# Fused linear attention and two MoE layers on one core: y of a step in one go, a new order of issue, and eight low parts moved to VectorE

## The chip, the cores and the metric

The kernel runs on one core of a Trainium2 chip. The metric is the device time of one execution in microseconds. Three executions of the kernel before took 455.67, 456.74 and 457.1 us, so the median is 456.74 us. The trace shown here is of a further execution of 458.59 us, whose span from the first to the last instruction is 456.7 us; 1.9 us lie around the span.

Five engines are named: PE (TensorE, matmuls; PEld is its loading of weights), DVE (VectorE), ACT (ScalarE), POOL (GpSimd) and SP (SyncE, which here only issues DMAs).

## The reference

Three layers follow each other, all in float32.

```
# 1. attention with a decaying state: batch 2, 8 heads, 768 positions, head_dim 48
for t in range(768):
    y[t]  = r[t] @ (state + (u*k[t]) outer v[t])
    state = w[t][:, None] * state + k[t] outer v[t]
x = y as 1536 tokens x 384
# 2. dense layer ("MoE1"): 384 -> 2048 -> 384
x = silu(x @ w_in) @ w_out
# 3. routed layer ("MoE2"): 8 experts, top 1, 384 -> 1024 -> 384
out[i] = gate[i] * (relu(x[i] @ w1[e]) @ w2[e])     e = argmax(x[i] @ w_gate)
```

## The kernel before, in words

**Attention.** The 1536 tokens are cut into 12 steps of 128 positions, the two batches alternating (step n belongs to batch n % 2). One step makes, from running products of w, scaled keys `kh` and scaled queries `rh`, and then: `kp` transposes kh, `Kt` copies it out of PSUM, `U` is keys times values, `sc` are scores between positions, `cp` and `cq` copy the scores under the mask into `A` (even and odd heads, written before with the diagonal by `Ad` and `Ae`), `Sb` updates the state, and `y` (three column groups j = 0, 1, 2) sums the part from the old state `Tb` and the part from `A`. `xh` and `xl` split y into a high and a low part. The tiles of w, of the running products (`QF`), of rk, kh, rh and Tb exist once, so a step reuses what the step before has read.

Up to now the y of a step was issued in two pieces: the token `y` (group 0: 16 matmuls from the third step on) and the token `z` (groups 1 and 2: 40 matmuls), with other work between them.

**The layers.** Tokens go through MoE1 in six chunks of 256, two attention steps each. A chunk is 8 units; a unit is `s1_` (18 matmuls into a PSUM bank), `gh` and `sg` (ACT: silu, twice), `gl` (DVE: low part) and `s2_` (12 matmuls that add into the chunk's sums). Every product is made of three passes: high x high, high x low, low x high. MoE1's 16 weight pieces come as 64-bit floats and are decoded: `drw` loads one, `wx` shifts its low word (L350 on ACT or L352 on DVE, as the letter in `L3` says), `wy` (DVE, L356), `wt` (ACT, L360) and `wo` (DVE, L364) build the float, `wh` (ACT, L368) rounds the high part and `wl` (L372, POOL or DVE as `LO` says) makes the low part. Four buffers hold pieces that are being decoded.

MoE2's weights come as float32: ACT rounds the high part (L386) and DVE or POOL subtracts it for the low part (L387). The first pieces are converted while MoE1's last chunk runs.

**Routing.** For each finished chunk c, `ra` and `rd` copy its sums into rows, `jk` (16 of them, DVE, L476) are the dot products with the gate's weights, `rt` finds the expert, `cu` (PE) counts, `ru_` (`gates`) makes slots and gate values, and `rs` (POOL) scatters the rows.

**What sets the order.** The string `PLAN` lists the work of PE, ACT, DVE and POOL in the order in which each engine takes it, from the start until MoE1's unit 31 of 48; a colon gives the PSUM banks. SP's loads keep the order in which they stand there too. What comes after PLAN (the rest of MoE1, MoE2) is put in order by the framework's scheduler from its own estimates; `REST` says which leftovers of routing are handed in at which slot there. Each engine takes its instructions strictly in order, so one that waits holds up all that stand behind it.

In the loop over units 32 to 47, `ensure(m, lo)` converts MoE2's pieces up to m; `lo` is the engine of the low parts. In the last chunk (`c == NCH - 1`) it is called at units i = 1, 2, 3 (pieces 0 to 7) and 4, 5 (pieces 8 to 11).

Of the kernel before, what the change touches and what calls it, by code (L numbers as in the profile page):

```python
# [36 lines left out]

L3 = "DAADADADADADADDA"  # L40
# [3 lines left out]
PLAN = """
dw0 drk0 dvv0 Qs0 drw0 pd0 PC0 kh0 Fs0 kp0:0 dw1 Kt0 ru0 drk1 jq0 U0:1 rh0 wx0 dvv1 dp0:2 Sb0 drw1 wy0 sc0:34 dg0 wt0 Qs1 Ad0 wo0 dw2 PC1 pd1 ru1 Ae0
drk2 cp0 y0:5 wh0 Fs1 dp1:6 wx1 cq0 wl0 z0 jq1 kh1 rh1 kp1:7 xh0 dvv2 dg1 wy1 Ad1 sc1:01 dtk2 xl0 Kt1 Qs2 Ae1 drw3 U1:2 cp1 wt1 pd2 cq1 PC2 y1:3 tk2
Sb1 z1 wo1 xh1 xl1 wh1 Fs2 s1_0:4 wl1 jq2 kh2 dw3 rh2 dg2 drk3 Tb2 kp2:6 Ad2 wx3 sc2:57 wy3 gh0 dvv3 Ae2 Qs3 dtk3 s1_1:0 sg0 cp2 Kt2 drw2 wt3 gl0 cq2
PC3 wo3 drw5 pd3 tk3 wh3 U2:1 gh1 y2:2 sg1 Sb2 wx2 wl3 z2 gl1 drw4 dg3 Fs3 lc xh2 s2_0:36 Ad3 drw7 xl2 jq3 kh3 rh3 kp3:4 Ae3 Tb3 sc3:57 wy2 dw4 Kt3
drk4 wx5 wx4 U3:1 cp3 wy5 y3:0 dvv4 wt2 cq3 dtk4 wt5 Sb3 z3 wo2 wo5 xh3 wh2 xl3 wh5 wl2 s1_8:2 wl5 drw6 wy4 s1_2:4 gh8 wx7 tk4 wt4 drw9 sg8 s2_1 gl8
gh2 wo4 sg2 wx6 gl2 s1_9:5 wy7 Qs4 wh4 s1_10:7 wt7 dg4 wl4 pd4 gh9 wx9 PC4 sg9 Ad4 wo7 s2_8:10 drw8 gl9 wh7 Fs4 Ae4 s1_3:2 wl7 gh10 jq4 kh4 drw11 s2_2  # L50
rh4 sg10 Tb4 wx8 gl10 wy6 kp4:4 sc4:57 wy9 gh3 Kt4 wy8 sg3 U4:4 wt6 gl3 wt9 cp4 Sb4 wt8 cq4 y4:2 wo6 s1_11:4 wo9 wh6 wo8 wh9 z4 wl6 wh8 s2_9 wx11 wl9
xh4 drw10 xl4 wl8 s1_4:5 gh11 drw13 wy11 sg11 gl11 wt11 s2_3 wo11 wx10 drw12 s1_5:7 gh4 wy10 wh11 wx13 sg4 s2_10 wl11 wt10 gl4 drw14 wo10 wx12 s2_4
wy13 gh5 wy12 s1_12:2 wh10 sg5 wl10 wt13 gl5 s2_11 wx14 wt12 wo13 drw15 gh12 sg12 wo12 wh13 s1_6:4 gl12 wh12 wl13 dw5 wl12 s1_13:5 drk5 gh6 wy14 sg6
wx15 gl6 dvv5 s2_5 Qs5 dtk5 wt14 wy15 s1_7:7 PC5 gh13 wo14 wt15 pd5 sg13 kh5 wh14 s2_12 gl13 tk5 kp5:2 gh7 wo15 s2_13 Kt5 sg7 Fs5 wh15 gl7 wl14 U5:4
jq5 dg5 s1_14:5 Ad5 dw6 wl15 Ae5 rh5 s2_6 Tb5 drk6 gh14 Sb5 sg14 Qs6 sc5:27 dvv6 gl14 PC6 dtk6 cp5 s2_7 pd6 cq5 Fs6 y5:4 ra0 s1_15:5 kh6 jq6 rd0 tk6
dw7 z5 gh15 sg15 dg6 kp6:2 rh6 xh5 s2_14 Ad6 gl15 drk7 xl5 Kt6 Tb6 Ae6 sc6:73 Qs7 dvv7 U6:6 dtk7 cp6 PC7 s1_16:5 pd7 cq6 Sb6 Fs7 y6:4 gh16 s1_17:2 kh7
sg16 jq7 tk7 gl16 dw8 z6 gh17 sg17 dg7 kp7:7 xh6 gl17 s2_15 Ad7 xl6 rh7 Kt7 Tb7 drk8 Ae7 sc7:36 Qs8 ra1 U7:5 cp7 dvv8 PC8 s1_18:2 rd1 dtk8 cq7 Sb7 pd8
y7:4 kh8 gh18 s2_16:71 Fs8 sg18 gl18 tk8 jq8 z7 dw9 kp8:0 xh7 rh8 s1_19:3 Kt8 xl7 drk9 dg8 Tb8 Ad8 sc8:65 Qs9 dvv9 gh19 U8:2 dtk9 Ae8 cp8 s2_17 pd9
sg19 Sb8 PC9 gl19 cq8 y8:0 Fs9 s1_20:4 kh9 jq9 tk9 z8 dw10 gh20 sg20 kp9:2 xh8 gl20 s2_18 Kt9 xl8 rh9 dg9 drk10 sc9:36 Tb9 Ad9 Qs10 U9:5 dvv10 Ae9 cp9
s1_21:4 dtk10 Sb9 PC10 cq9 pd10 y9:2 kh10 gh21 s2_19 Fs10 sg21 gl21 tk10 jq10 z9 dw11 kp10:0 rh10 xh9 s1_22:5 Kt10 dg10 drk11 xl9 Ad10 Tb10 sc10:36  # L60
Qs11 dvv11 gh22 Ae10 U10:4 dtk11 cp10 sg22 s2_20 pd11 PC11 cq10 lw0 gl22 Sb10 s1_23:0 Fs11 lf0 kh11 jq11 s2_21 tk11 gh23 sg23 gl23 kp11:2 y10:3 dg11
Kt11 s1_24:6 jk0_0 Ad11 jk0_1 lw1 jk0_2 Ae11 jk0_3 z10 jk0_8 jk0_9 gh24 jk0_10 lf1 sg24 U11:5 rh11 xh10 s2_22 gl24 xl10 Tb11 jk0_4 sc11:40 Sb11 jk0_5
s1_25:2 cp11 jk0_6 cq11 y11:6 jk0_7 gh25 s2_23 jk0_11 sg25 jk0_12 gl25 jk0_13 z11 jk0_14 ra2 jk0_15 rd2 s1_26:3 xh11 rt0 xl11 jk1_0 cu0:5 gh26 jk1_1
s2_24:40 sg26 ru_0 s1_27:2 gl26 rs0 jk1_2 jk1_3 jk1_4 s2_25 gh27 jk1_5 jk1_6 sg27 jk1_7 gl27 s1_28:7 jk1_8 jk1_9 jk1_10 jk1_11 s2_26 gh28 jk1_12 sg28
jk1_13 jk1_14 gl28 s1_29:1 jk1_15 rt1 s2_27 gh29 jk2_0 jk2_1 sg29 jk2_2 gl29 cu1:6 jk2_3 s1_30:5 ru_1 s2_28 gh30 jk2_4 rs1 jk2_5 sg30 jk2_6 gl30
s1_31:3 jk2_7 jk2_8 jk2_9 jk2_10 s2_29 gh31 jk2_11 sg31 jk2_12 jk2_13 gl31 s1_32:2 jk2_14 jk2_15 rt2 s2_30 gh32 sg32 gl32 cu2:7 s1_33:1 ru_2 s2_31
"""
# [1091 lines left out]
```

## Time and profile before

| | |
|---|---|
| median of three runs | 456.74 us |
| profiled execution | 458.59 us, span 456.7 us |
| PE busy | 427.9 us, 94% of the span |
| DVE busy | 307.4 us, 67% |
| ACT busy | 229.3 us, 50% |
| POOL busy | 150.8 us, 33% |
| mean granted PE clock | 0.963 |

A line of the chain that ended last, or of a timeline, begins with the start in us from the span's start and a duration in us. In lists of groups the number after the bar is the sum in us, and the next one the mean duration of one in ns. Matmuls overlap: from one to the next counts the difference of their starts, not the duration. PE's granted clock has two levels: 1.00 stands for 2.4 GHz and 0.50 for 1.2 GHz.

### The profile page before, as it was taken

The page shows a single profiled execution, that of the slowest core. Times are in us where ns is not written, and L with a number is a line of the kernel's source. Part 1 is how long each engine was busy: PE and PEld are TensorE (multiplying, and loading weights), DVE is VectorE, ACT ScalarE, POOL GpSimd, SP SyncE. Part 2 cuts the span into 40 slices and gives each one's busy share as a digit, 9 for nine tenths or more (in the row PEclk, how much of TensorE's full clock was granted, in tenths as well). Part 3 has the DMA queues.
Part 4 walks back from the last instruction along what each step waited for, and adds up shares of the span by engine and source line. Part 5 has one row for each costly group of instructions (what it writes and reads, how often), then busy time and mean ns, then how long its engine had stood idle before and what let it go on. Part 6 is the DMA issues. An engine that isn't in the chain of part 4 may idle for free.

```text
span 456.7 us, 9042 instructions
## 1 busy us (share of the span) xinstructions
PE 427.9 (94%) x3551; PEld 406.9 (89%) x3551; DVE 307.4 (67%) x618; ACT 229.3 (50%) x438; POOL 150.8 (33%) x152
## 2 busy tenths in 40 slices
...
GB/s 270 389 155 164 154 202 148 254 186 194 195 133 130 104 152 183 135 35 36 3 35 36 1 69 209 165 187 243 244 207 255 205 201 245 213 112 27 0 32 33
DMA packets 20772, 67.83 MB, mean 149 GB/s; under 512 B 3042, under 2 KB 7293, under 8 KB 20720
## 3 DMA queue, kind: packets, MB, share of 16 engines
...
q14 instruction: 22, 0.18, 0.1%
...
## 4 chain that ended last, share of the span: by engine, by line
PE 62%; DVE 14%; issue 10%; DMA 7%; POOL 3%; ACT 2%; SPq 0%; POOLq 0%; DVEq 0%; ACTq 0%
PE s L400 27%; PE acc L429 23%; DMA rawd<-wd 4%; DVE jk L476 3%; PE acc L550 3%; PE y L304 3%; PE sc L273 2%; DVE rawd L364 2%; DVE QF L200 2%; POOL wt L372 1%; DMA tk<-tk 1%; PE U L288 1%; PE kp L261 1%; DVE A L278 1%; DMA rk<-rk 1%
## 5 line engine op out<-in xcount | busy, mean ns | idle before, releaser
L400 PE MATMUL s<-xh,wt 128*128 128x256 f32 x960 | 156.8, 286 | 4.4 <-DVE gl L420 2.7
L429 PE MATMUL acc<-wt,gh 128*128 128x384 f32 x576 | 149.7, 342 | 3.1 <-POOL wt L372 2.4
L400 PEld LDWEIGHTS s<-xh,wt 128*128 128x128 f32 x960 | 135.0, 191 | 7.0 <-DVE gl L420 2.9
L406 ACT ACTIVATE gh<-s 128x512 fp32r<-128x512 f32 x80 | 47.9, 598 | 125.3 <-PE s L400 115.0
L429 PEld LDWEIGHTS acc<-wt,gh 128*128 128x128 f32 x576 | 101.6, 190 | 4.5 <-POOL wt L372 2.6
L429 PE MATMUL acc<-wt,gl 128*128 128x384 f32 x288 | 95.9, 338 | 0.0
L400 PE MATMUL s<-xl,wt 128*128 128x256 f32 x480 | 84.1, 284 | 0.8 <-DVE xl L332 0.7
L387 POOL TENSOR_TENSOR wt<-raw,wt 128x768 fp32r<-128x768 f32 x34 | 64.4, 1900 | 60.6 <-ACT wt L386 60.5
L400 PEld LDWEIGHTS s<-xl,wt 128*128 128x128 f32 x480 | 69.1, 191 | 1.4 <-DVE xl L332 1.2
L386 ACT CAST wt<-raw 128x768 fp32r<-128x768 f32 x64 | 52.7, 834 | 15.9 <-PE acc L429 11.9
L429 PEld LDWEIGHTS acc<-wt,gl 128*128 128x128 f32 x288 | 54.4, 190 | 0.3 <-DVE gl L420 0.3
L420 DVE TENSOR_TENSOR gl<-s,gh 128x512 fp32r<-128x512 f32 x48 | 32.9, 686 | 31.4 <-ACT s L409 31.0
L387 DVE TENSOR_TENSOR wt<-raw,wt 128x768 fp32r<-128x768 f32 x30 | 33.8, 1131 | 26.2 <-ACT wt L386 25.9
L422 DVE SCALAR_TENSOR_TENSOR gl<-s,gh 128x512 fp32r<-128x512 f32 x32 | 22.1, 691 | 38.9 <-ACT gh L406 38.8
L476 DVE SCALAR_TENSOR_TENSOR jk<-xr,wgr 128x384 f32<-128x384 f32 x80 | 46.9, 640 | 0.0
L204 POOL TENSOR_TENSOR tk<-tk 128x384 f32<-128x384 f32 x10 | 12.2, 1219 | 72.1 <-DMA tk<-tk 56.0
L252 ACT ACTIVATE A<-ident,dg 128x128 f32<-128x128 f32 x96 | 30.4, 393 | 3.6 <-DVE dg L243 2.7
...
L409 ACT ACTIVATE s<-s 128x512 f32<-128x512 f32 x48 | 28.4, 593 | 0.0
L372 POOL TENSOR_TENSOR wt<-rawd,wt 128x768 fp32r<-128x768 f32 x5 | 11.4, 2289 | 46.6 <-ACT wt L368 46.6
L304 PE MATMUL y<-A,vv 128*32 128x128 f32 x384 | 17.8, 286 | 4.4 <-DVE A L278 3.6
L278 DVE COPY_PREDICATED A<-mask,sc 128x512 f32<-128x512 int32 x24 | 17.5, 728 | 5.2 <-PE sc L273 5.0
...
## 6 DMA issues: line engine op xcount, KB each, us to landing
...
```

The costliest lines, as they stand in the source:

```text
L252: nc.scalar.activation(out=d["A"][:, h], in_=ident, func=AF.Copy, scale=d["dg"][:, h:h + 1])
L278: nc.vector.copy_predicated(d["A"][:, h::2], bc(mask.bitcast(I32).unsqueeze(1), [128, 4, 128]), d["sc"][h])
L304: nc.tensor.matmul(d["y"][ps_, j], l, r, start=i == (1 if n < B else 0), stop=i == len(a[j]))
L386: nc.scalar.copy(t[:, 0], r)
L387: lo.tensor_tensor(out=t[:, 1], in0=r, in1=t[:, 0].bitcast(F32), op=ALU.subtract)
L400: nc.tensor.matmul(s[:, fi], wv[:, a, k, fi * 128:fi * 128 + 128], x[b][:, k], start=n == 0, stop=n == 8)
L406: lz["sg"] = nc.scalar.activation(out=gt[u][0], in_=gt[u][2], func=f)
L409: lz["sg"] = nc.scalar.activation(out=gt[u][2], in_=gt[u][2], func=AF.Silu)
L420: nc.vector.tensor_tensor(out=gl, in0=s, in1=gh.bitcast(F32), op=ALU.subtract)
L422: nc.vector.scalar_tensor_tensor(out=gl, in0=s, scalar=0.0, in1=gh.bitcast(F32), op0=ALU.max, op1=ALU.subtract)
L429: lz["s2"] = nc.tensor.matmul(acc[j][:, 0:DM], g[a][:, fi, j * 128:j * 128 + 128], w[:, b, fi * DM:fi * DM + DM], start=first and fi == 0 ...
L476: nc.vector.scalar_tensor_tensor(out=jk, in0=ro[c]["xr"][j][:, 0:DM], scalar=1.0, in1=wgr[e // 4][:, e % 4], op0=ALU.mult, op1=ALU.mult, a ...
```

## The change

1. From the third step on (`ONE_Y = 2`) the token `y` issues all 56 matmuls of a step's y; the tokens z2 to z11 are gone.
2. `PLAN`, `REST` and `BANKS` are new. The attention's step 4, which stood among the decoding of MoE1's weights, now comes after it, so that steps 4 to 11 stand where steps 5 to 11 stood. On PE, s2_0 stands behind kp3, sc3 and U3, and U2 stands ahead of s1_1. On DVE, Fs2 stands ahead of xl1, Fs3 ahead of gl0, and wy2, wy5 and wx4 ahead of xl3. SP's loads for step 4 come after the last of MoE1's weights. The last dot products, expert choice and gates of chunk 2 (jk2_15, rt2, cu2, ru_2) go from PLAN to REST.
3. `L3` is D throughout: the shift `wx` of all 16 pieces is made by DVE (eight were made by ACT).
4. `ensure(2 * i + 1)` at units 1 to 3 of the last chunk: the low parts of MoE2's pieces 0 to 7 are made by DVE (POOL made them).

```diff
-L3 = "DAADADADADADADDA"
+RUN = 2
+
+ONE_Y = 2
+
+L3 = "DDDDDDDDDDDDDDDD"
...
-Sb1 z1 wo1 xh1 xl1 wh1 Fs2 s1_0:4 wl1 jq2 kh2 dw3 rh2 dg2 drk3 Tb2 kp2:6 Ad2 wx3 sc2:57 wy3 gh0 dvv3 Ae2 Qs3 dtk3 s1_1:0 sg0 cp2 Kt2 drw2 wt3 gl0 cq2
-PC3 wo3 drw5 pd3 tk3 wh3 U2:1 gh1 y2:2 sg1 Sb2 wx2 wl3 z2 gl1 drw4 dg3 Fs3 lc xh2 s2_0:36 Ad3 drw7 xl2 jq3 kh3 rh3 kp3:4 Ae3 Tb3 sc3:57 wy2 dw4 Kt3
-drk4 wx5 wx4 U3:1 cp3 wy5 y3:0 dvv4 wt2 cq3 dtk4 wt5 Sb3 z3 wo2 wo5 xh3 wh2 xl3 wh5 wl2 s1_8:2 wl5 drw6 wy4 s1_2:4 gh8 wx7 tk4 wt4 drw9 sg8 s2_1 gl8
...
+Sb1 z1 wo1 xh1 Fs2 wh1 xl1 jq2 wl1 s1_0:4 dw3 kh2 rh2 dg2 drk3 Tb2 Ad2 wx3 wy3 kp2:6 dvv3 Ae2 sc2:57 Qs3 dtk3 gh0 Kt2 pd3 sg0 drw2 Fs3 U2:0 wt3 PC3
+s1_1:1 gl0 jq3 cp2 tk3 drw5 Sb2 cq2 gh1 sg1 y2:2 wo3 drw4 gl1 wh3 kh3 xh2 rh3 kp3:3 xl2 wl3 sc3:64 Kt3 dg3 wx2 Ad3 U3:0 wx5 lc drw7 Tb3 s2_0:57 Ae3
+cp3 Sb3 cq3 wy2 y3:1 wy5 wt2 wx4 wt5 wo2 xh3 wo5 wh2 xl3 wh5 wl2 s1_8:2 wl5 drw6 wy4 s1_2:3 gh8 wx7 wt4 wy7 drw9 sg8 wo4 s2_1 wt7 gl8 gh2 wh4 wo7
...
 REST = """
-gh33 sg33 gl33 rs2 ra3 rd3 jk3_0 jk3_1 jk3_2 jk3_3 jk3_4 jk3_5 jk3_6 jk3_7 jk3_8 jk3_9 jk3_10 jk3_11 jk3_12 jk3_13 jk3_14 jk3_15 rt3 cu3:0 ru_3 rs3
+gh33 sg33 gl33 jk2_15 rt2 ra3 rd3 jk3_0 jk3_1 cu2:1 jk3_2 ru_2 rs2 jk3_3 jk3_4 jk3_5 jk3_6 jk3_7 jk3_8 jk3_9 jk3_10 jk3_11 jk3_12 jk3_13 jk3_14 jk3_15
+rt3 cu3:1 ru_3 rs3
...
-BANKS = (3, 7, 4, 0, 6, 5, 2, 1)
+BANKS = (4, 2, 0, 1, 6, 7, 5, 3)
...
-"y": lambda n, b: at6(n, 0, b[0]),
+"y": lambda n, b: (at6(n, 0, b[0]), at6(n, 1), at6(n, 2)) if n >= ONE_Y else at6(n, 0, b[0]),
...
         if c == NCH - 1 and 1 <= i < 4:
-            ensure(2 * i + 1, nc.gpsimd)
+            ensure(2 * i + 1)
```

## Rows read from the trace of the kernel before

**Rows 1.** Stretches of the span: length, busy us (instructions), PE clock, DMA share, GB/s

```profile
24.00:52.40 28.40, 21.49 (x255) 17.91 (x254) 24.66 (x41) 18.37 (x40) 8.71 (x30) 0.88 0.45 160
52.40:229.00 176.60, 174.45 (x1640) 164.13 (x1641) 151.04 (x321) 98.85 (x207) 39.99 (x42) 1.00 0.42 139
...
262.70:275.60 12.90, 12.90 (x109) 12.75 (x107) 12.85 (x21) 6.18 (x10) 10.22 (x5) 1.00 0.18 61
...
279.80:286.60 6.80, 6.18 (x32) 6.18 (x32) 2.66 (x16) 3.60 (x8) 2.17 (x3) 0.50 0.65 264
```

**Rows 2.** Timeline of VectorE from 262.6 us

```profile
267.22 2.19 DVE L476 SCALAR_TENSOR_TENSOR jk<-xr,wgr 128x384 f32<-128x384 f32 x1
...
269.35 0.68 DVE L420 TENSOR_TENSOR gl<-s,gh 128x512 fp32r<-128x512 f32 x1
...
277.63 0.68 DVE L420 TENSOR_TENSOR gl<-s,gh 128x512 fp32r<-128x512 f32 x1
...
280.19 0.17 DVE L490 TENSOR_TENSOR oh<-cd,cm 128x16 bf16<-128x16 f32 x1
```

**Rows 3.** Timeline of GpSimd from 256 us

```profile
266.87 8.50 POOL L387 TENSOR_TENSOR wt<-raw,wt 128x768 fp32r<-128x768 f32 x4 [2.39 <-ACT wt L386]
```

**Rows 4.** Timeline of TensorE, 275 to 287 us

```profile
278.37 0.62 PE L400 MATMUL s<-xh,wt 128*128 128x256 f32 x3 [2.71 <-DVE gl L420]
...
286.43 0.62 PE L400 MATMUL s<-xh,wt 128*128 128x256 f32 x3
```

**Rows 5.** Groups of VectorE, 220 to 262.6 us

```profile
L476 DVE SCALAR_TENSOR_TENSOR jk<-xr,wgr 128x384 f32<-128x384 f32 x17 | 8.4, 553 | 0.0
```

**Rows 6.** Timeline of ScalarE from 256 us

```profile
283.91 1.57 ACT L386 CAST wt<-raw 128x768 fp32r<-128x768 f32 x2 [3.20 <-DMA raw<-wpc]
```

**Rows 7.** Timeline of TensorE, first 62 us

```profile
36.05 0.43 PE L304 MATMUL y<-rh,Tb 128*32 128x128 f32 x8
...
36.51 0.40 PE L304 MATMUL y<-rh,Tb 128*32 128x128 f32 x8
...
41.76 0.69 PE L429 MATMUL acc<-wt,gh 128*128 128x384 f32 x1 [2.37 <-POOL wt L372]
```

**Rows 8.** TensorE in the stretch before its clock fell

```profile
37.46:40.88 3.42, 1.24 (x33) 1.00 0.27 77
```

**Rows 9.** Timeline of TensorE, 128.5 to 134.5 us: one step's y in two pieces

```profile
129.44 0.43 PE L304 MATMUL y<-rh,Tb 128*32 128x128 f32 x8
...
130.01 0.62 PE L400 MATMUL s<-xh,wt 128*128 128x256 f32 x3
...
132.35 0.42 PE L304 MATMUL y<-rh,Tb 128*32 128x128 f32 x8
```

**Rows 10.** Timeline of TensorE, 172 to 177 us: s1 between two s2

```profile
173.84 0.52 PE L400 MATMUL s<-xh,wt 128*128 128x256 f32 x3
...
175.98 0.51 PE L429 MATMUL acc<-wt,gh 128*128 128x384 f32 x2
```

**Rows 11.** Timeline of TensorE, 115 to 119.5 us: y5 waits

```profile
117.33 0.43 PE L304 MATMUL y<-rh,Tb 128*32 128x128 f32 x8
...
118.85 0.62 PE L400 MATMUL s<-xh,wt 128*128 128x256 f32 x3
```

**Rows 12.** Groups of VectorE, 24 to 112 us

```profile
L356 DVE SCALAR_TENSOR_TENSOR rawd<-rawd 128x768 uint32<-128x768 uint32 x14 | 13.1, 956 | 0.5 <-ACT rawd L350 0.4
...
L372 DVE TENSOR_TENSOR wt<-rawd,wt 128x768 fp32r<-128x768 f32 x10 | 9.3, 944 | 0.0
...
L352 DVE TENSOR_SCALAR rawd<-rawd 128x768 uint32<-128x768 uint32 x7 | 5.6, 801 | 1.8 <-DMA rawd<-wd 1.8
```

**Rows 13.** Chain that ended last, 55 to 120 us

```profile
106.53 2.92 DVE QF L200
...
109.47 1.16 ACT w L255 x2
...
111.25 4.17 DMA w<-wp
```

More of the change, by code (lines that the diff above doesn't have):

```diff
@@ L45 @@
 dw0 drk0 dvv0 Qs0 drw0 pd0 PC0 kh0 Fs0 kp0:0 dw1 Kt0 ru0 drk1 jq0 U0:1 rh0 wx0 dvv1 dp0:2 Sb0 drw1 wy0 sc0:34 dg0 wt0 Qs1 Ad0 wo0 dw2 PC1 pd1 ru1 Ae0
-drk2 cp0 y0:5 wh0 Fs1 dp1:6 wx1 cq0 wl0 z0 jq1 kh1 rh1 kp1:7 xh0 dvv2 dg1 wy1 Ad1 sc1:01 dtk2 xl0 Kt1 Qs2 Ae1 drw3 U1:2 cp1 wt1 pd2 cq1 PC2 y1:3 tk2
-Sb1 z1 wo1 xh1 xl1 wh1 Fs2 s1_0:4 wl1 jq2 kh2 dw3 rh2 dg2 drk3 Tb2 kp2:6 Ad2 wx3 sc2:57 wy3 gh0 dvv3 Ae2 Qs3 dtk3 s1_1:0 sg0 cp2 Kt2 drw2 wt3 gl0 cq2
-PC3 wo3 drw5 pd3 tk3 wh3 U2:1 gh1 y2:2 sg1 Sb2 wx2 wl3 z2 gl1 drw4 dg3 Fs3 lc xh2 s2_0:36 Ad3 drw7 xl2 jq3 kh3 rh3 kp3:4 Ae3 Tb3 sc3:57 wy2 dw4 Kt3
@@ L49 @@
-drk4 wx5 wx4 U3:1 cp3 wy5 y3:0 dvv4 wt2 cq3 dtk4 wt5 Sb3 z3 wo2 wo5 xh3 wh2 xl3 wh5 wl2 s1_8:2 wl5 drw6 wy4 s1_2:4 gh8 wx7 tk4 wt4 drw9 sg8 s2_1 gl8
-gh2 wo4 sg2 wx6 gl2 s1_9:5 wy7 Qs4 wh4 s1_10:7 wt7 dg4 wl4 pd4 gh9 wx9 PC4 sg9 Ad4 wo7 s2_8:10 drw8 gl9 wh7 Fs4 Ae4 s1_3:2 wl7 gh10 jq4 kh4 drw11 s2_2
-rh4 sg10 Tb4 wx8 gl10 wy6 kp4:4 sc4:57 wy9 gh3 Kt4 wy8 sg3 U4:4 wt6 gl3 wt9 cp4 Sb4 wt8 cq4 y4:2 wo6 s1_11:4 wo9 wh6 wo8 wh9 z4 wl6 wh8 s2_9 wx11 wl9
-xh4 drw10 xl4 wl8 s1_4:5 gh11 drw13 wy11 sg11 gl11 wt11 s2_3 wo11 wx10 drw12 s1_5:7 gh4 wy10 wh11 wx13 sg4 s2_10 wl11 wt10 gl4 drw14 wo10 wx12 s2_4
@@ L53 @@
[L53 to L64, printed above, removed]
@@ L65 @@
-jk1_13 jk1_14 gl28 s1_29:1 jk1_15 rt1 s2_27 gh29 jk2_0 jk2_1 sg29 jk2_2 gl29 cu1:6 jk2_3 s1_30:5 ru_1 s2_28 gh30 jk2_4 rs1 jk2_5 sg30 jk2_6 gl30
-s1_31:3 jk2_7 jk2_8 jk2_9 jk2_10 s2_29 gh31 jk2_11 sg31 jk2_12 jk2_13 gl31 s1_32:2 jk2_14 jk2_15 rt2 s2_30 gh32 sg32 gl32 cu2:7 s1_33:1 ru_2 s2_31
+drk2 cp0 y0:5 wh0 Fs1 dp1:6 cq0 jq1 wl0 z0 kh1 rh1 kp1:7 xh0 dvv2 dg1 wx1 Ad1 sc1:01 xl0 dtk2 wy1 Kt1 Ae1 drw3 Qs2 U1:2 wt1 cp1 PC2 pd2 y1:3 tk2 cq1
+Sb1 z1 wo1 xh1 Fs2 wh1 xl1 jq2 wl1 s1_0:4 dw3 kh2 rh2 dg2 drk3 Tb2 Ad2 wx3 wy3 kp2:6 dvv3 Ae2 sc2:57 Qs3 dtk3 gh0 Kt2 pd3 sg0 drw2 Fs3 U2:0 wt3 PC3
@@ new lines @@
+s1_1:1 gl0 jq3 cp2 tk3 drw5 Sb2 cq2 gh1 sg1 y2:2 wo3 drw4 gl1 wh3 kh3 xh2 rh3 kp3:3 xl2 wl3 sc3:64 Kt3 dg3 wx2 Ad3 U3:0 wx5 lc drw7 Tb3 s2_0:57 Ae3
+cp3 Sb3 cq3 wy2 y3:1 wy5 wt2 wx4 wt5 wo2 xh3 wo5 wh2 xl3 wh5 wl2 s1_8:2 wl5 drw6 wy4 s1_2:3 gh8 wx7 wt4 wy7 drw9 sg8 wo4 s2_1 wt7 gl8 gh2 wh4 wo7
+s1_9:0 sg2 wx6 wl4 wh7 gl2 wx9 s1_10:6 drw8 gh9 wl7 sg9 wy6 s1_3:4 gl9 wt6 drw11 wy9 wo6 wt9 s2_2 wh6 wo9 wl6 wh9 s2_8:12 wx8 gh3 drw10 wl9 sg3 wx11
+gl3 s2_9 gh10 wy8 sg10 drw13 wy11 wt8 gl10 s1_4:3 wt11 wo8 wo11 wh8 s2_3 wx10 gh4 wl8 wh11 sg4 wy10 drw12 s1_5:0 gl4 wt10 wl11 wo10 s1_11:4 drw14 gh5
@@ new lines @@
+wx13 sg5 wh10 wy13 s2_4 gl5 wl10 wt13 wx12 s1_12:6 wo13 drw15 gh11 sg11 wy12 wh13 gl11 s2_10 wt12 wl13 dw4 wo12 drk4 s1_6:3 wx14 gh12 wh12 wy14 dvv4
+sg12 wl12 wt14 s2_5 dtk4 gl12 wo14 wx15 s1_7:0 wh14 Qs4 gh6 sg6 wy15 PC4 s2_11 gl6 wl14 wt15 pd4 s1_13:4 gh7 wo15 sg7 Fs4 wh15 s2_6 gl7 tk4 jq4 dw5
+s1_14:6 gh13 wl15 sg13 kh4 gl13 kp4:3 rh4 s2_7 Kt4 dg4 drk5 Tb4 Ad4 Qs5 sc4:04 ra0 dvv5 gh14 pd5 U4:3 rd0 Ae4 dtk5 cp4 s2_12 Sb4 sg14 PC5 gl14 cq4
+s1_15:5 Fs5 kh5 jq5 y4:7 tk5 gh15 dw6 sg15 kp5:3 gl15 s2_13 xh4 rh5 Kt5 xl4 drk6 dg5 sc5:60 Tb5 Ad5 Qs6 dvv6 U5:4 Ae5 cp5 dtk6 s2_14 Sb5 PC6 cq5 pd6
@@ new lines @@
+y5:5 kh6 Fs6 kp6:3 xh5 Tb6 s2_15 jq6 rh6 xl5 tk6 Kt6 dw7 sc6:74 ra1 rd1 U6:6 drk7 dg6 s1_16:0 Ad6 Sb6 dvv7 Qs7 Ae6 dtk7 s1_17:5 cp6 gh16 pd7 PC7 sg16
+cq6 gl16 y6:3 gh17 Fs7 sg17 kh7 jq7 s1_18:1 gl17 tk7 xh6 dw8 xl6 kp7:2 gh18 s2_16:67 rh7 Kt7 dg7 sg18 drk8 Tb7 Ad7 gl18 sc7:40 Qs8 dvv8 Ae7 U7:5 dtk8
+cp7 PC8 s1_19:3 Sb7 cq7 pd8 kh8 y7:2 gh19 Fs8 sg19 gl19 tk8 kp8:1 jq8 s2_17 Kt8 dw9 rh8 xh7 U8:5 dg8 drk9 xl7 sc8:40 Ad8 Tb8 s1_20:3 Qs9 dvv9 Ae8 dtk9
+cp8 PC9 Sb8 s2_18 gh20 cq8 sg20 pd9 gl20 y8:1 Fs9 kh9 jq9 s1_21:2 rh9 xh8 Tb9 dw10 tk9 xl8 drk10 kp9:5 gh21 sc9:40 Kt9 sg21 U9:3 dvv10 dg9 gl21 Ad9
@@ new lines @@
+s2_19 dtk10 Sb9 Qs10 Ae9 s1_22:1 cp9 PC10 pd10 cq9 tk10 s2_20 gh22 sg22 gl22 y9:5 Fs10 kh10 jq10 s1_23:2 dg10 rh10 xh9 dw11 Ad10 Tb10 xl9 drk11 kp10:3
+gh23 sc10:40 Ae10 dvv11 s2_21 cp10 sg23 dtk11 Qs11 Kt10 U10:1 gl23 lw0 PC11 cq10 s1_24:5 Sb10 pd11 tk11 lf0 y10:3 gh24 sg24 gl24 s2_22 xh10 Fs11 xl10
+jq11 s1_25:2 kh11 rh11 lw1 dg11 Tb11 kp11:4 Ad11 jk0_0 sc11:01 jk0_1 gh25 jk0_2 lf1 s2_23 Ae11 cp11 jk0_3 sg25 cq11 Kt11 gl25 U11:5 jk0_4 y11:3 jk0_5
+Sb11 jk0_6 s1_26:4 xh11 jk0_7 jk0_8 xl11 jk0_9 s2_24:01 ra2 jk0_10 gh26 jk0_11 rd2 sg26 jk0_12 s1_27:2 gl26 jk0_13 jk0_14 jk0_15 s2_25 gh27 rt0 sg27
```

11 lines of the change are left out of this document (7 added, 4 removed).

## The prediction

> **What bounds the kernel now.** I read the busy shares by stretch first [rows 1]. The reader is to see three kinds of stretch. From 52.4 us on TensorE is full (174.45 of 176.60 us busy): what this stretch costs is the sum of the matmuls, and other engines count only where TensorE waits for them. From 24 to 52.4 us it is not full (21.49 of 28.40). And behind 275.6 us it stands, and then runs at half its clock from 279.8 to 286.6 us (0.50, the 1.2 GHz level). Next I read TensorE's timeline at these places: a wait of 2.71 us for gl ahead of 278.37 [rows 4], one of 2.37 us for a low part by GpSimd ahead of 41.76 [rows 7]. Last I read what stands on the engines waited for [rows 2, 3]. So four terms decide.
>
> **Term 1: low parts by VectorE, 262 to 300 us.** GpSimd makes four low parts without a pause from 266.87 to 275.37 (8.50 us) [rows 3]. In the same time the dot product at 267.22 takes 2.19 us, where 17 others have a mean of 553 ns [rows 5]; five of the 16 are stretched so. The 16 start every 0.48 us where nothing disturbs them, 7.7 us; here, with two gl of 0.6 us, they fill 263.22 to 279.3, so some 7.2 us are lost. The gl whose input was there at 270.4 (end of its silu) runs at 277.63 [rows 2], and TensorE, which needs its PSUM bank, stands from 275.62 to 278.37 [rows 4].
>
> In their place come four low parts of 0.94 us [rows 12], 3.8 us, that fall in the same stretch (their high parts are rounded from 265.97 on); two more come before it, where VectorE idles, and two after. So the experts are found (oh) 3.4 us before 280.19, and the gl in question is behind seven dot products and at most four low parts: 270.7 to 274.3, ahead of 275.62. TensorE then does from 275.62 on without a stop what it did until 286.43: 18 + 18 matmuls and the counting, 2.15 + 2.15 + 0.14 = 4.4 us for 10.8. That is 6.4 us, 3.4 of it for the half clock that the stop brought on. I don't take all: ScalarE's next silu stood behind two roundings that waited 3.20 us for a load until 283.91 [rows 6]. The load was issued behind the 12th dot product (276.8); that ends about 5 us sooner, so roundings end near 280.5 and their gl near 282.5, where TensorE wants it at 282. I charge 1.1 us: **-5.3 us**. Ends: 0 (low parts stand ahead of the gl, and the stop stays) and -6.4.
>
> **Term 2: fewer changes on TensorE.** An s1 between y and z takes 130.01 to 132.35, 2.34 us [rows 9]; between two s2 it takes 2.14 [rows 10]. So a change between full and quarter-width matmuls costs 0.10 us. From s1_8 to the end of PLAN the old order has 53 of them (a change to kp is free and not counted), the new one 37: 16 x 0.10 = 1.6 us less. In one go y's first group takes 0.46 us to the next start [rows 7], alone 0.57 [rows 9]: 8 steps x 0.11 = 0.9. Added up block by block, with the unrounded costs, it is **-2.4 us**. This holds only where TensorE is full. Ends: -1 and -2.6.
>
> **Term 3: waits from 52 to 229 us.** Step 4's y, U and state cost 1.1 us of standing (70 to 75 us), y5 stands 117.33 to 118.85, 1.5 for 0.57 us [rows 11], and cu2 another 0.8 at 223.6: 2.9 us in all. Step 4 leaves the decoding (7 us of VectorE's time), cu2 goes to the scheduler, and y5 comes when decoding is over. But eight steps now stand where seven stood, 10.9 us of TensorE's work apart, and 47 dot products with their routing, 36 us of VectorE, come in the last 40 us of PLAN. I take half as new waits: **-1.5 us**, ends -2.9 and +2.
>
> ScalarE to VectorE for eight shifts (0.80 us each, 6.4 us [rows 12]) I cost at nothing here: the stretch in which they fall loses step 4's 7 us. The Trainium skill speaks against it (Perfetto Trace Analysis, "Optimizing Scalar/DVE Operations"): when VectorE is saturated, work should go from it to ScalarE. VectorE is busy 151 of 176.6 us here [rows 1], TensorE 174, so the trace does not yet bear it out; the rule has its place among the rivals.
>
> **Term 4: the start, 20 to 52 us.** For: kp3, sc3 and U3 now stand where TensorE waited 2.37 us [rows 7]; Fs3 and pd3 move into VectorE's 1.2 us of waiting for w3 ahead of 34.05, so kh3 comes 1 to 2 us sooner. Adding up VectorE's queue, s1_8 gets going up to 3.0 us earlier. Against: xl1 is 1.4 us later behind Fs2, and xl3 stands behind wy2, wy5 and wx4 (0.96 + 0.96 + 0.80 us [rows 12]) while TensorE has three matmuls. That is a gap of some 3 us. Before the old gap at 37.46 to 40.88 TensorE had 1.24 of 3.42 us busy [rows 8], and its clock fell to 0.50 for the next 6.8 us. One such fall in the full stretch costs 3.4. I take gain and loss as even: **0**, ends -3.0 and +3.9.
>
> SP's loads for step 4 pass behind eight of MoE1's weights; nothing asks for them until decoding ends, and the weights come sooner for it. POOL loses tk4 from among its low parts and eight low parts of MoE2; nothing there waits.
>
> **Sum.** -5.3 - 2.4 - 1.5 + 0 = -9.2 us on the profiled 458.59, so 449.4. That execution lies 1.85 us above the median, so beside the runs shown the forecast is 447.5 us, 445 to 450.5 for this case alone. All good ends together give 456.74 - 14.9 = 441.8.
>
> **Rivals.**
> *Low parts take the place of the block.* On VectorE, in strict order, they stand ahead of gl or wait for a rounding that waits for a load. For: ScalarE's 3.20 us [rows 6]. Against: VectorE needs 7.7 + 3.8 + 1.8 us of the 16 from 263. Term 1 shrinks to -1: 451.8 us.
>
> *A second fall of the clock* in the start, by the gap ahead of xl3. For: the same share of work before the old fall [rows 8]; against: my gap is a sum of a dozen terms. 447.5 + 3.4 = 450.9. The skill has it as a rule (TensorE: Matmul & The Clock Gate, "What's actually happening"): half rate is the default and activity lifts it. Both falls in this trace agree.
>
> *VectorE paces the decoding*, as the skill's rule has it: the eight shifts are paid in full, 447.5 + 6.4 = 453.9.
>
> *Slower: the attention's loop.* Buffers of w and QF exist once, so step n + 1 begins only when the square of step n is done and a new w has landed. The chain shows one round from 106.53: scan, square at 109.47, load 111.25 to 115.42, then the next scan [rows 13]: 8.9 us and then a queue. The new order asks for one step each 10.9 us, seven times over. If a round takes 12.3 us in VectorE's queue, TensorE stands 1.4 us in each, 7 x 1.4 = 9.8, and the gain is gone: 457.3 and, with the clock that such stops bring down, 460. It decides from 12.2 us (9.2 / 7 + 10.9). Against: from 129 to 163 us three rounds of 11.1 ran without any wait.
>
> **Chances.** Forecast 0.52; second fall 0.15; low parts in place of the block 0.14; decoding 0.05; better than 445 us 0.06; the loop 0.08. What can't be told from no change is 0.3%, 1.4 us: faster is all below 455.4, 0.88 with a part of mixed cases taken off; same 0.04; slower 0.08. The range runs from 443.5 to 453.5: it takes in the two likely rivals.
>
> **What would show it.** Term 1: all dot products near 0.55 us after 262, no wait of TensorE for gl there, clock 1.00 throughout; wrong if a wait for gl or wt of over 2 us stays. Term 2: s1 after s1 of 2.15 us, y of 1.7 in one piece. Term 3: TensorE's waits from 52 to 221 us under 1.5 us. Term 4: the time of s1_8 against 53.7 and where the clock falls. Wrong as a whole if VectorE's share beside TensorE's waits rises in the last third of PLAN.

## The result and the profile after

The changed kernel takes 450.34 us (median of four, 448.47 to 451.28) beside 456.63 us of the kernel before: 6.3 us less by the medians. The ratio of the times is given as 0.9851, 95% interval 0.9822 to 0.9879, which is 5.5 to 8.1 us. Six more executions had a median of 450.9 us (0.9869, 0.9825 to 0.9913). The forecast was 447.5 us, in the range 443.5 to 453.5.

The two profiled executions are further apart than the medians: 458.59 us is above all four times of before in that comparison, 448.47 us is the fastest of its four. In their timelines the 10 us are found here:

| from TensorE's timeline, us | before | after | difference |
|---|---|---|---|
| start of s1_2 | 55.60 | 55.04 | -0.6 |
| from there to the first matmul of the last chunk's sums (L550, now L555) | 209.10 | 204.87 | -4.2 |
| those sums, first to last | 34.67 | 28.15 | -6.5 |
| from there to MoE2's first s1 (the rows) | 6.80 | 8.51 | +1.7 |
| from there to the last instruction | 150.59 | 150.20 | -0.4 |

Line numbers after are larger by 5. Busy time by stretch, columns as in [rows 1]; the five busy times are those of PE, PEld, DVE, ACT and POOL, in this order. The stretches are the start, the full stretch up to s2_31, the last chunk, and the rows (the routing of the last tokens, up to MoE2's first s1):

```profile
24.00:52.40 28.40, 20.06 (x259) 17.46 (x259) 27.86 (x44) 17.73 (x39) 7.38 (x28) 0.94 0.48 161
52.40:221.00 168.60, 167.80 (x1617) 161.38 (x1616) 149.35 (x308) 92.73 (x197) 41.23 (x42) 1.00 0.44 146
254.60:288.10 33.50, 33.50 (x279) 33.46 (x278) 24.85 (x68) 17.41 (x29) 2.70 (x6) 1.00 0.31 107
288.10:296.60 8.50, 7.07 (x52) 6.04 (x50) 4.23 (x22) 3.03 (x9) 0.39 (x2) 1.00 0.79 286
```

In the full stretch TensorE stands 0.8 us, where it stood 2.15 [rows 1]. In the last chunk it is busy for all 33.5 us at 1.00; the stop and the half clock are gone. In the rows it stands 1.4 us.

VectorE in the last chunk, its groups and then its timeline (against [rows 5] and [rows 2]):

```profile
L392 DVE TENSOR_TENSOR wt<-raw,wt 128x768 fp32r<-128x768 f32 x12 | 11.3, 954 | 0.1
L481 DVE SCALAR_TENSOR_TENSOR jk<-xr,wgr 128x384 f32<-128x384 f32 x16 | 8.2, 555 | 0.0
```

```profile
274.25 0.69 DVE L425 TENSOR_TENSOR gl<-s,gh 128x512 fp32r<-128x512 f32 x1 [0.36 <-ACT s L414]
...
275.74 0.17 DVE L495 TENSOR_TENSOR oh<-cd,cm 128x16 bf16<-128x16 f32 x1
...
280.27 2.69 DVE L392 TENSOR_TENSOR wt<-raw,wt 128x768 fp32r<-128x768 f32 x3
282.88 0.21 DVE L523 CAST si<-sl 128x1 int32<-128x1 f32 x2
```

The 16 dot products now have a mean of 555 ns, and gl waits for its silu alone. The experts (oh) are not found sooner: 15.8 us behind the first matmul of the sums, where it was 15.5 [rows 2]. From the first dot product to oh it takes 16.6 us, where it took 17.0: six low parts of 0.95 us and four gl now stand between, where there were no low parts and two gl, and they take up what the dot products gave back. The sums end 6.5 us sooner, so this chain now ends last. And look at 280.27: three low parts stand ahead of `si`, the cast of the slot numbers, which needs 0.1 us for each of its two parts and whose input was there. The chain that ended last shows what hangs on it (start, us, what):

```profile
282.01 0.95 DVE wt L392
282.96 0.12 DVE si L523 x2
...
283.79 1.02 POOL xs L537
...
285.12 2.71 DMA xs<-xr,si
...
287.94 3.75 DMA er<-xs
...
291.74 1.56 PE xg L607 x6
```

GpSimd's timeline has the same from its side, and TensorE's the stop (against [rows 3] and [rows 4]):

```profile
276.00 0.19 POOL L507 TENSOR_TENSOR r<-run,oh 128x8 bf16<-128x8 bf16 x1 [32.00 <-DVE oh L495]
...
283.79 1.02 POOL L537 DMA_INDIRECT xs<-xr,si  x1 [7.32 <-DVE si L523]
```

```profile
291.74 1.56 PE L607 MATMUL xg<-zi,er 128*128 128x256 f32 x6 [1.16 <-DMA er<-xs]
```

ScalarE's roundings no longer wait for a load, where one waited 3.20 us [rows 6]:

```profile
279.55 0.83 ACT L391 CAST wt<-raw 128x768 fp32r<-128x768 f32 x1 [0.27 <-PE acc L555]
```

The start, and one y in one go (against [rows 7] and [rows 9]); y takes 152.43 to 154.10, 1.67 us:

```profile
35.02 1.13 PE L293 MATMUL U<-vv,Kt 128*128 128x96 f32 x8 [2.44 <-ACT Kt L270]
41.62 0.63 PE L266 MATMUL kp<-ident,kh 128*128 128x128 f32 x4 [1.62 <-DVE kh L237]
43.78 1.47 PE L278 MATMUL sc<-rh,kh 64*128 64x128 f32 x16 [1.53 <-DVE rh L242]
...
53.15 0.61 PE L405 MATMUL s<-xl,wt 128*128 128x256 f32 x3 [0.55 <-DVE xl L337]
```

```profile
152.43 0.43 PE L309 MATMUL y<-rh,Tb 128*32 128x128 f32 x8
...
154.10 0.62 PE L405 MATMUL s<-xh,wt 128*128 128x256 f32 x3
```

The wait for GpSimd's low part ahead of 41.76 is gone; waits for VectorE's kh and rh and for Kt stand in its place. Between 24 and 52.4 us the clock falls to 0.50 once, for 3.4 us from 44.49 on (it was 6.83 us from 40.88 on). That difference is not the new start's doing: with the cast first (below), which leaves the start as it is, the half clock lasts 6.83 us from 42.78 on.

### The profile page after: what moved, and what is told of

It is laid out like the page before. It is cut to its first block, busy times and chain, and to the rows that moved or that the text cites. A ratio compares the mean times of both kernels' runs of the same rounds, so it can differ in the third digit from the quotient of the medians.

```text
span 446.8 us, 9032 instructions
## 1 busy us (share of the span) xinstructions
PE 419.9 (94%) x3551; PEld 403.5 (90%) x3551; DVE 310.4 (69%) x634; ACT 223.1 (50%) x430; POOL 134.8 (30%) x144
## 4 chain that ended last, share of the span: by engine, by line
PE 73%; DVE 10%; issue 9%; DMA 4%; POOL 1%; ACT 1%; SPq 0%; POOLq 0%; ACTq 0%; DVEq 0%
PE s L405 33%; PE acc L434 28%; PE y L309 2%; PE acc L555 2%; PE U L293 2%; PE sc L278 2%; DMA w<-wp 2%; DVE QF L205 2%; DVE A L283 1%; DMA rk<-rk 1%; POOL out L537 1%; DVE rawd L369 1%; PE tp L653 1%; DMA er<-xs 1%; DVE rawd L361 1%
## 5 line engine op out<-in xcount | busy, mean ns | idle before, releaser
L405 PE MATMUL s<-xh,wt 128*128 128x256 f32 x960 | 155.0, 284 | 1.4 <-ACT xh L331 1.2
L392 POOL TENSOR_TENSOR wt<-raw,wt 128x768 fp32r<-128x768 f32 x26 | 48.6, 1874 | 40.5 <-ACT wt L391 40.4
L392 DVE TENSOR_TENSOR wt<-raw,wt 128x768 fp32r<-128x768 f32 x38 | 41.5, 1096 | 25.9 <-ACT wt L391 25.7
L481 DVE SCALAR_TENSOR_TENSOR jk<-xr,wgr 128x384 f32<-128x384 f32 x80 | 40.8, 554 | 0.0
L414 ACT ACTIVATE s<-s 128x512 f32<-128x512 f32 x48 | 28.4, 591 | 0.0
L537 POOL DMA_INDIRECT xs<-xr,si x12 | 12.6, 1052 | 32.3 <-DVE si L523 11.9
```

The source lines that it names most:

```text
L392: lo.tensor_tensor(out=t[:, 1], in0=r, in1=t[:, 0].bitcast(F32), op=ALU.subtract)
L405: nc.tensor.matmul(s[:, fi], wv[:, a, k, fi * 128:fi * 128 + 128], x[b][:, k], start=n == 0, stop=n == 8)
L414: lz["sg"] = nc.scalar.activation(out=gt[u][2], in_=gt[u][2], func=AF.Silu)
L481: nc.vector.scalar_tensor_tensor(out=jk, in0=ro[c]["xr"][j][:, 0:DM], scalar=1.0, in1=wgr[e // 4][:, e % 4], op0=ALU.mult, op1=ALU.mult, a ...
L537: i = nc.gpsimd.indirect_dma_start(out=dst, out_offset=bass.IndirectOffsetOnAxis(ap=idx, axis=0), in_=src, in_offset=None, bounds_check=bo ...
```

## The experiments

All times are medians; before is 456.6 to 457.5 us in every comparison. Theory: the four terms of the forecast. Rivals: a term is given back elsewhere, or is the clock's.

**Low parts on GpSimd again.**

```diff
-            ensure(2 * i + 1)
+            ensure(2 * i + 1, nc.gpsimd)
```

> The changed kernel with its fourth part undone: the low parts of MoE2's pieces 0 to 7 on GpSimd again. Theory (GpSimd's low parts stretch VectorE's dot products and so stop TensorE): dot products of about 2 us come back, TensorE stands 2 to 3 us for gl in the last chunk of MoE1, its clock falls for 6.8 us there, and the time rises by 4.5 to 5.5 us to about 455. Rival (the gain in that stretch comes from the new order, which merely shifted it in time): the time stays within 1.4 us of 450.3.

454.62 us (0.9942 of before, 0.9916 to 0.9968), 4.1 more than the 450.57 of all ten executions of the changed kernel. VectorE's groups in the last chunk, lines of GpSimd's and VectorE's timelines, and TensorE's timeline there:

```profile
L481 DVE SCALAR_TENSOR_TENSOR jk<-xr,wgr 128x384 f32<-128x384 f32 x16 | 15.0, 991 | 0.0
L425 DVE TENSOR_TENSOR gl<-s,gh 128x512 fp32r<-128x512 f32 x7 | 4.8, 689 | 7.0 <-ACT s L414 7.0
```

```profile
265.90 8.50 POOL L392 TENSOR_TENSOR wt<-raw,wt 128x768 fp32r<-128x768 f32 x4 [2.39 <-ACT wt L391]
```

```profile
268.38 0.68 DVE L425 TENSOR_TENSOR gl<-s,gh 128x512 fp32r<-128x512 f32 x1
...
270.50 2.20 DVE L481 SCALAR_TENSOR_TENSOR jk<-xr,wgr 128x384 f32<-128x384 f32 x1
```

```profile
277.40 0.92 PE L405 MATMUL s<-xh,wt 128*128 128x256 f32 x3 [2.71 <-DVE gl L425]
```

The mean of the dot products rises from 555 to 991 ns, 7.0 us for 16: five of them are stretched, to 2.2 us at most. The stop of 2.71 us is back, with a half clock from 277.53 on, for 3.41 us and not the 6.8 expected. gl is not stretched: the one at 268.38, amid GpSimd's four low parts, takes 0.68 us. One of its two inputs, s, is in PSUM; both of a dot product's are in SBUF. The Trainium skill has this as a rule (SBUF — State Buffer, "Who interferes with whom"): a VectorE instruction with two SBUF inputs contends with a GpSimd instruction that reads SBUF, one with at most one, outside VectorE's two-port modes, does not. This trace agrees with both halves.

**Low parts alone, in the kernel before.**

```diff
-            ensure(2 * i + 1, nc.gpsimd)
+            ensure(2 * i + 1)
```

> The kernel before with only the fourth part of the change: low parts of pieces 0 to 7 by VectorE. Theory: the stretch is 4.8 us shorter, as between the two profiles, and the time is 451.5 to 452.5. Rival (this part pays only beside the new order): within 1.4 us of 456.6.

456.04 us (0.9982, 0.9953 to 1.0011): a gain of 1.0 us by the medians, 2.1 us at most by the interval, and a miss. The last chunk shrank in full, 34.67 to 28.15. What came behind took it back. TensorE's waits from 288 to 330 us, and SP's (us in total, times, longest us):

```profile
PE tp L648 <- DMA er<-xs: 2.2, 1, 2.2
PE xg L602 <- DMA er<-xs: 1.8, 1, 1.8
```

```profile
SPq L629 <- DMA xs<-xr,si: 4.6, 1, 4.6
```

The rows took 9.15 us instead of 6.80, and 13 us later the second expert's rows were 2.2 us late. The scatter that they wait for landed 6.4 us after its issue (3.6 before, 4.0 in the changed kernel), among five loads of 768 KB issued from 293.97 us on; the changed kernel has as many there, so what made it late is not settled. Behind the second wait TensorE ran 3.41 us at half clock; half of that, 1.7 us, is taken as lost. 2.35 + 2.2 + 1.7 = 6.25 us of the 6.5 gained.

**The cast of the slot numbers first, in that kernel and in the changed one.** The same edit in both:

```diff
-        lz["r4"] = nc.vector.tensor_reduce(sl.unsqueeze(2), p2, AX.X, ALU.add)
+        nc.vector.tensor_reduce(sl.unsqueeze(2), p2, AX.X, ALU.add)
+        si = d["si"] = [rt.tile([128, 1], I32, name=f"si{j}", bufs=2) for j in range(2)]
+        for j in range(2):
+            lz["r4"] = nc.vector.tensor_copy(si[j], d["sl"][:, j:j + 1])
...
     def r4b(c):
         d = ro[c]
-        si = d["si"] = [rt.tile([128, 1], I32, name=f"si{j}", bufs=2) for j in range(2)]
-        for j in range(2):
-            nc.vector.tensor_copy(si[j], d["sl"][:, j:j + 1])
```

> The kernel before, with two edits: the low parts of the last chunk by VectorE, as in the change, and the two casts of the slot numbers (si) moved ahead of them on VectorE. Theory (the low parts alone gained only 1.0 us because their gain is given back behind them: TensorE waits 2.35 us more ahead of the rows, and 2.2 us for the second expert's rows, since scatters and row loads come late and among more weight loads): both waits shrink, the rows are there within 7.5 us of the last chunk's end, 450.5 to 453. Rival (the give-back is the weight loads themselves, which start earlier and fill the DMA queues whenever the low parts free their buffers early): the first wait goes, the second stays or moves, 453.5 to 455. Second rival (nothing there matters, the loss is the clock's): 455.5 or more.

> The changed kernel, with the two copies that turn slots into whole numbers (si) right behind the slots, ahead of three low parts of pieces 8 to 11 that VectorE makes there. Theory (GpSimd's scatter of chunk 4 waited for si behind these low parts, so MoE2's first rows came 1.2 us late for TensorE): the scatter starts about 2.6 us sooner, TensorE's wait for the rows goes, and the time falls by 1.2 to 1.8 us to about 448.7. Rival (the rows' DMA is late for another reason, such as the loads of weights beside it): no change.

> The changed kernel with the two casts of the slot numbers ahead of the low parts, once more, beside the changed kernel itself on the same chip. Theory (TensorE's wait of 0.8 to 1.3 us ahead of the rows goes, and with it a fall of the clock in some executions): 0.8 to 1.8 us less than the changed kernel of this call. Rival (what is saved at the rows is lost to the start's half clock): the same within 0.5 us.

In the kernel before with the low parts moved: 453.47 us (0.9923, 0.9894 to 0.9952), 2.6 less than without the cast moved, half a microsecond above the theory's span. The wait for the second expert's rows is gone, of the first 0.8 us are left. In the changed kernel: 449.40 us (0.9846, 0.982 to 0.9872), 0.9 less than its first four and so short of the 1.2 expected; and 448.53 us (0.9818, 0.9774 to 0.9861) beside 450.9 of the changed kernel in the same comparison, 2.4 less and more than the 1.8 expected. All twelve executions against all ten: 449.33 against 450.57 us, 1.2 less (0.1 to 2.3 by their scatter). VectorE's timeline, then the rows by stretch:

```profile
281.77 0.21 DVE L520 CAST si<-sl 128x1 int32<-128x1 f32 x2
281.91 3.55 DVE L392 TENSOR_TENSOR wt<-raw,wt 128x768 fp32r<-128x768 f32 x4
```

```profile
289.50:296.50 7.00, 6.78 (x50) 5.88 (x49) 4.18 (x22) 2.99 (x9) 0.39 (x2) 1.00 0.95 337
```

TensorE's wait for er is gone, and 8.5 us are 7.0. This version is faster than both kernels, than the changed one by little more than the scatter.

**The shifts on ScalarE again.**

```diff
-L3 = "DDDDDDDDDDDDDDDD"
+L3 = "DAADADADADADADDA"
```

> The changed kernel with eight of the 16 shifts of MoE1's low words on ScalarE again, the order of the tokens unchanged. Theory (the shifts cost nothing, their cover is TensorE's work): within 1.4 us of 450.3. Rival (VectorE is what ends last from 24 to 52 us, where it was busy 27.5 of 28.0 us in the changed kernel): without the shifts of pieces 1, 2 and 4 the first unit behind step 3 starts 1 to 2 us sooner and the time is 448.5 to 449.5. A third outcome, slower by 1 us or more, would mean that ScalarE's queue is what ends last there.

450.43 us (0.9853, 0.9828 to 0.9877): the same as the changed kernel. So the eight shifts cost VectorE nothing that shows in the time.

**y in one go, alone.** Two kernels: the order of before without z2 to z11, y at its old place or at the place of z. (At the old place y3 stands ahead of cq3, so part of its scores are not under the mask yet.)

```diff
-"y": lambda n, b: at6(n, 0, b[0]),
+"y": lambda n, b: (at6(n, 0, b[0]), at6(n, 1), at6(n, 2)) if n >= 2 else at6(n, 0, b[0]),
...
-U3:1 cp3 wy5 y3:0 dvv4 wt2 cq3 dtk4 wt5 Sb3 z3 wo2 wo5 xh3
+U3:1 cp3 wy5 dvv4 wt2 cq3 dtk4 wt5 Sb3 y3:0 wo2 wo5 xh3
```

> The kernel before, with y of steps 2 to 11 in one go and nothing else changed: the order is the old one without the z entries. Theory (TensorE is full from 52 us on, so each of 8 steps saves 0.11 us of its first group and some 9 of the 47 changes between full and quarter-width matmuls go, 0.10 us each): 1.8 us less, 454.5 to 455.6. Rival (the y in one go holds TensorE while the next unit's silu or low part is awaited, or its gain is hidden by such waits): 456 to 458, no gain without the new order.

> The kernel before, with y of steps 2 to 11 in one go at the place where its second part stood (so that all its scores are there); nothing else changed. Theory (the matmul sums of the forecast hold in the old order too: 8 x 0.11 us and 13 of 47 changes of 0.10 us): 2.2 us less than before, 454 to 455.3. Rival (in the old order the one block is hidden by or turned into waits, as with y at its earlier place, 458.17): 456 to 458.

At the old place 458.17 us (1.0013, 0.9985 to 1.004), no gain; at the place of z 455.39 us (0.996, 0.9928 to 0.9991), 1.8 us less by the ratio and 2.1 by the medians. TensorE's timeline, y at the old place and then at the place of z:

```profile
50.20 0.63 PE L400 MATMUL s<-xh,wt 128*128 128x256 f32 x3 [0.60 <-ACT xh L326]
53.57 1.01 PE L400 MATMUL s<-xl,wt 128*128 128x256 f32 x3 [2.74 <-DVE xl L332]
```

```profile
52.35 0.62 PE L400 MATMUL s<-xl,wt 128*128 128x256 f32 x3 [0.74 <-DVE xl L332]
```

At the old place y3 and xh3 are ready early and s1_8 begins, but xl3 still stands on VectorE behind a copy of scores, the state and two float builds: a gap of 2.74 us, and from 52.21 on 6.83 us at half clock. From the start of s1_8 to that of s1_9 it takes 11.90 us, at the place of z 7.50: 2.0 us more for the gap and 2.4 us for the clock. That hides a gain that is there. The gap comes in part from the order itself: the second copy of scores (cq3) overwrites what y3 reads, and in the first old-start kernel below, which has the same order there, it waits 1.19 us for y.

**y in two parts, in the changed kernel.** The second part stands just ahead of xh.

```diff
-ONE_Y = 2
+ONE_Y = 12
...
-s1_18:1 gl17 tk7 xh6
+s1_18:1 gl17 tk7 z6 xh6
```

> The changed kernel, with y of steps 2 to 11 in two parts again, the second part just ahead of its xh in the new order; all else as changed. Theory (matmul sums): 8 x 0.11 us and 8 more changes of 0.10 us each come back, +1.7 us, 451.5 to 452.7. Rival (the second part now stands behind a full block and delays xh, so that s1 waits): 453 or more. Second rival (y in one go is worth nothing, the order does it): 449.9 to 450.9.

456.78 us (1.0002, 0.9973 to 1.0031): 6.2 more than the changed kernel, and the first rival by its time, though no wait of over 0.1 us here is for xh, as that rival had it. The stretch from s1_2 to the last chunk takes 210.50 us, 5.6 more than in the profile after. Its waits there (us in total, times, longest us):

```profile
PE U L293 <- ACT Kt L270: 1.1, 2, 0.7
PE kp L266 <- DVE kh L237: 1.0, 1, 1.0
PE sc L278 <- DVE rh L242: 0.4, 1, 0.4
PE y L309 <- DVE pd L196: 0.4, 1, 0.4
```

They are 2.9 us where the changed kernel has 0.3 from 56 us on. The rest is TensorE's own work. Four profiles show this for the stretch from s1_2 to the last chunk (length, TensorE's busy us, clock, DMA share, GB/s): before, after, y in two parts in the changed kernel, and y alone at the place of z.

```profile
55.60:264.70 209.10, 207.69 (x1884) 1.00 0.36 120
55.04:259.91 204.87, 204.62 (x1884) 1.00 0.37 123
55.64:266.14 210.50, 207.53 (x1884) 1.00 0.35 118
54.25:261.12 206.87, 204.85 (x1883) 1.00 0.36 121
```

Two parts cost TensorE 2.9 us of work (207.53 against 204.62) and 2.7 of waits, which is all of the 5.6; the theory's 1.7 us of work was too small. In the old order one go saves the same work (207.69 to 204.85). In the rows it lost another 1.65 us: 10.16 us, with a half clock from 297.92 on.

**The old start.** The order of before up to s1_8, without step 4's loads, the rest as changed; first with y2 and y3 in one go (y3 ahead of cq3 as above) and all shifts on VectorE, then with both as before. The end of that part of PLAN, and what the second has besides:

```diff
-U3:0 wx5 lc drw7 Tb3 s2_0:57 Ae3 cp3 Sb3 cq3 wy2 y3:1 wy5 wt2 wx4 wt5 wo2 xh3 wo5 wh2 xl3 wh5 wl2 s1_8:2
+U3:0 cp3 wy5 y3:1 wt2 cq3 wt5 Sb3 wo2 wo5 xh3 wh2 xl3 wh5 wl2 s1_8:2
...
-ONE_Y = 2
+ONE_Y = 4
-L3 = "DDDDDDDDDDDDDDDD"
+L3 = "DAADADADADADADDA"
```

> The changed kernel with the order of issue of the kernel before up to s1_8 (some 53 us), less step 4's loads and with y in one go; everything behind as changed. Theory (gain and loss of the new start are even; where the half clock falls there differs from run to run anyhow): within 1 us of the changed kernel, 449.5 to 451.5. Rival (the new start halves the half-clock stretch near 41 us, 3.4 for 6.8 us, and that is worth 1.7 us or more): 452 or more, with a stretch of 6.8 us in the profile. Second rival (the new start is a loss): 449 or less.

> The changed kernel with the shifts and, up to s1_8, the order of issue of the kernel before; y of steps 2 and 3 in two parts there as before, step 4's loads left where the change puts them; everything behind s1_8 as changed. Theory (the two starts are even, and the 4.6 us that the old start lost with all shifts on VectorE came from those shifts and from y3 in one go, ahead of its xl): 449.5 to 451.5. Rival (the new order of the start is worth those 4.6 us): 453.5 to 455.5, with s1_8 later than 53 us and a stretch at half clock near 41 us of 6.8 us.

454.91 us (0.9939, 0.9909 to 0.9969) and 450.29 us (0.984, 0.9795 to 0.9884). The second says that the two starts are even. The first lost 4.6 us. The half clock near 42 us is 6.83 us long in its profile, as the rival said, but 3.41 in the second's, so it goes with the execution and not with the start. Its stretch behind s1_8, beside the same of the second:

```profile
55.56:62.39 6.83, 5.95 (x28) 5.95 (x29) 5.74 (x9) 3.51 (x6) 0.00 (x0) 0.50 0.59 195
```

```profile
55.56:62.39 6.83, 6.83 (x54) 6.83 (x53) 5.33 (x9) 6.74 (x11) 1.90 (x1) 1.00 0.53 214
```

It is the gap of y3 in one go again (2.75 us of waiting for xl3, in both kernels that have it), and not mainly the shifts that I named first. From s1_8 to s1_9 the first takes 12.10 us and the second 7.50, and these are the 4.6 us: 2.0 of them more waiting for xl3, 2.6 the half clock.

**The changed kernel once more.**

> The changed kernel itself, beside the one with the casts moved: 449.5 to 451.3 as in its first runs, and a second profile of it to see which of its stretches differ from one execution to the next. Theory (its first profile, 448.47, was one of its fastest): a later first unit of full-width s1 than 53 us, or a half-clock stretch more, accounts for the difference. Rival: the stretch behind 229 us differs.

450.9 us (449.06 to 452.62). The profiled execution, 449.06 us, was again the fastest, with s1_2 at 54.52 and every later stage within 0.8 us of the profile after. So neither the theory nor its rival is tested: what an execution of 452 us has more is not seen here.

## Why the forecast came out, by its steps

The sum was -9.2 us; measured are -6.3 by the medians. The direction was right, and so were the mechanisms of terms 1 and 2; the size was 2.8 us off, 1.2 of it in term 1 and 1.0 in term 3, and the rest lies within the scatter.

- **Term 1, low parts by VectorE: -5.3; measured -4.1** (2.7 to 5.1 by the scatter of ten executions of each). The mechanism is shown by the kernel with the low parts back on GpSimd: stretched dot products, gl late, stop, half clock. The last chunk came out just past the far end of my range (-6.5), and the 1.1 us that I charged for a late load did not arise. Some 1.3 of the 6.5 hang on the one profile of before: with y in one go alone the last chunk, with GpSimd still on it, takes 33.35 us, and its half clock lasts 3.41 instead of 6.83 us. The step that failed is "So the experts are found (oh) 3.4 us before 280.19": relative to the last chunk they came 0.3 us later, since six low parts and four gl stood ahead of them, not four and two, and three low parts behind them stand ahead of si, on which scatter, row load and TensorE hang: +1.7 us. I had followed gl and not this chain. With the cast first, the kernels stand 5.3 us apart (454.62 to 449.33).
- **Term 2, fewer changes on TensorE: -2.4; measured some -2.6.** TensorE's busy time from s1_2 to the last chunk is 207.16 to 207.75 us in three profiles of the old order with y in two pieces, and 204.62 to 205.29 us in seven of the new order; 204.85 in the old order with y in one go. As time, y in one go alone gave 1.8 us in the old order (interval 0.4 to 3.3), for that kernel waits 2.0 us there, where the three wait 0.5 to 1.5. Counted by the shapes of the tiles, PLAN behind s1_8 has 48 changes before and 32 after, not my 53 and 37; the difference, 16, is the same.
- **Term 3, waits: -1.5; measured some -0.5.** In the seven profiles of the new order TensorE waits 0.3 to 0.9 us in that stretch, where the three of the old order have 0.5 to 1.5; the whole stretch takes a mean of 205.6 us. (The kernel with the old start and y3 in one go is not among the seven, because its half clock lasts into the stretch.) The term was mis-sized: I set 2.9 us of standing to be won, and the profile of before has 1.4 us of it from s1_2 on, 2.15 with what lies ahead [rows 1]. The 0.8 us that I counted for cu2 at 223.6 was no standing, for TensorE made four s2 matmuls there (the line stands below this list). In the changed kernel these four stand behind s2_31, which is 0.7 of the 1.0 us by which that part is longer (38.87 us up to the last chunk, 37.90 before). The new order was not run without the rest of the change, so this term is a difference of profiles.
- **Shifts on VectorE: 0; measured 0.** The Trainium skill's rule on a saturated VectorE (Perfetto Trace Analysis, "Optimizing Scalar/DVE Operations"), priced at 453.9 us, did not decide: VectorE is busy 149.35 of 168.6 us, and the time is the same with the shifts on ScalarE.
- **Term 4, the start: 0; measured 0**, by the old start put back. The gap ahead of xl3 that I feared came at 0.55 us here; it came at 2.74 us, with the fall of the clock that I priced at 3.4 us, where y3 was fused in the old order, ahead of cq3.
- **The rivals.** Low parts in the place of the block: not in the last chunk, but in a place that I had not named. The loop of the attention: the steps' y run from 110.86 to 187.03 us without a wait of over 0.3 us. With y in two parts the time, 456.78 us, is near that rival's 457.3, but not by its mechanism: the waits are 2.9 us in all, not 9.8. The second fall, priced at 450.9, lies next to the measured time, yet neither profile of the changed kernel has it. The kernel with the low parts back on GpSimd, whose start is the same, has one of 3.41 us from 55.66 on, and its s1_2 begins at 57.67 us: the fall comes in single executions.

TensorE in the kernel before, at the place of cu2 (term 3):

```profile
223.67 0.95 PE L429 MATMUL acc<-wt,gh 128*128 128x384 f32 x4
```

What stays open: by its stages the kernel with GpSimd's low parts should stand 2.7 us above the changed one (4.45 in the last chunk less 1.72 in the rows), and its median stands 4.1 above; and why single executions of the changed kernel reach 452 us. Two candidates, neither seen in such an execution, are that second fall and a fall in the rows, which take 10.04 us with it in the second old-start kernel, 8.51 without.
